# Moving PSUM evictions and a table's sign turns from VectorE to ScalarE, and one batch's stages by two slots, in a fused FFT filter and FFN kernel

## The chip, the cores and the metric

The kernel runs on one core of a Trainium2 chip. The metric is the device time in microseconds of one execution, as the median of several. TensorE, VectorE, ScalarE, GpSimd and SyncE are called PE, DVE, ACT, POOL and SP, as in the profile; L302 is line 302 of the kernel before.

## The reference

`x` is (8, 3008, 256): 8 batches, 3008 positions, 256 channels. Each channel is filtered along the positions by way of a Fourier transform, and each of the 24064 tokens then goes through a feed-forward layer:

```python
X = np.fft.rfft(x, axis=1)
Y = X * (filt_r + 1j * filt_i)[None, :, :]
y = np.fft.irfft(Y, n=3008, axis=1).reshape(24064, 256)
h = y @ w_in                                  # 256 x 2048
g = 0.5 * h * (1.0 + erf(h / np.sqrt(2.0)))
out = g @ w_out                               # 2048 x 256
```

## The kernel before

One class, `_Mix`, holds the tiles and the stages. The program writes the order of the instructions out by hand (`manual_schedule`): what is issued first stands first in the queue of its engine.

**The transform.** 3008 is split into 47 × 64, and each batch goes through two short transforms with tables on the partitions, the product with the filter between them, and two more short transforms. For batches 1 to 7 the stages are: `s1` (4 units; matmuls at L397, evictions into `a_sb`, a DMA to DRAM `R1`), `r1` (a DMA back as `b_sb`, L416), `s2` (12 units; matmuls at L424, and on DVE the product with the filter `F` into `p`, L427), `s3` (3 units; matmuls at L441 into four PSUM banks; `s3_out` evicts them into `v_sb`, two at once and two one slot later, and starts a DMA to `R2`), `r2` (a DMA back as `d_sb`) and `s4` (16 units: 8 groups `grp` by 2 halves; matmuls at L469, eviction into the ring `y_sb`). A stage takes PSUM banks from pool "f" (3 banks), a few from pool "h" (3 banks, shared with `mm1`).

**Evictions.** `_evac` (L299) copies a PSUM tile to SBUF: ACT where its argument is "act" (L302), else DVE (L304, or L306 with a factor). Before, `s3_out` gives the tile of `par` 0 to DVE and that of `par` 1 to ACT (L451); `s4` gives half 0 to DVE and half 1 to ACT (L474).

**The prologue** does batch 0 with stages of its own (`c1`, `c1t`, `c2`, `c3`, `c3t`, `c4`) and builds the tables. Table 3 has three quarters of eight columns, `q` 0 to 2. `table_3` transposes a quarter on PE into a PSUM bank, and `table_3_copy` lets ACT copy it to `T3`; a second table, `T3i`, is the same with its two parts swapped and signs turned by a per-partition factor (`turn_r`, `turn_i`). Before, quarters 0 and 1 get this from `table_3_turn` (L289: two DVE instructions that read `T3`), quarter 2 from ACT out of PSUM (L283). `c2` multiplies on DVE with the filter rows (L513); the rows on partitions 64 to 127 are copied there by `dup_filters` (L117), mostly on POOL. `c3` (L531) reads `T3` and `T3i`.

**The main loop** has 47 token tiles of 512 tokens, 16 slots each. In a slot stand, in this order: what `put` has entered for the slot, some matmuls of the second layer for the tile before (`mm2_seven`, L657), and one unit of the first layer (`mm1`: two matmuls, L584, and the GELU on ACT, L587). The second layer is done in seven products instead of eight, for which DVE adds and subtracts quarters of `g_sb` (`sums_1` L626, `sums_2` L632, `sums_3` L639) and puts the products together (L672 to L686).

In tile 5 (slots 80 to 95) batch 1's tokens begin during the tile, so its first six slots have no `mm1` but 14 matmuls of `mm2_seven` each, and the ten others hold all 16 `mm1`.

Where a batch's stages stand is given by a few numbers for each batch: `s1`, `r1`, `s2`, `r2`, `s4` are first slots, `n1`, `n2`, `n4` distances, `group` the distance between groups of four `s2` units. `hi` is the slot where the batch's tokens begin, 176 for batch 2.

```python
unit = lambda p: s2 + group * (p // 4) + int(n2 * (p % 4))
for p in range(12):
    put(unit(p), m.s2, b, p)
    if p % 4 == 3:
        put(unit(p) + 3, m.s3, b, p // 4)
        put(unit(p) + 4, m.s3_out, b, p // 4, 1)
```

`r1` of the last chunk follows the fourth unit of s2 by one slot, and the loads of the next batch's `x`, with a small POOL instruction (`gate`) that reads a `p`, stand in the slots of `s2` units.

Of the kernel before, what the change touches and what calls it, by code (L numbers as in the profile page):

```python
# [30 lines left out]
class _Mix:  # L31
# [244 lines left out]
    def table_3_copy(self, q, turn):  # L276

        k = slice(8 * q, 8 * q + 8)
        self._evac(self.T3[:, k], self.t3.rearrange("p (k w e) -> p k e w", k=8, e=4), "act")
        if turn:  # L280
            v = self.t3.rearrange("p (k w h r) -> p k h r w", k=8, h=2, r=2)
            for r in range(2):
                self._evac(self.T3i[:, k, r::2, :], v[:, :, :, 1 - r, :], "act", self.turn[r])  # L283
# [163 lines left out]
    def s3_out(self, b, u, i):  # L447
        ps = self.st[b, "ps3"][i]
        vt = self.pv.tile([128, 4, 256], BF16, tag="v", name="v_sb")
        for par in range(2):  # L450
            self._evac(vt[:, 2 * par:2 * par + 2, :].rearrange("p a b -> p (a b)"), ps[par], "act" if par else False)  # L451
        for q in range(2):
            self.nc.sync.dma_start(out=self.st[b, "R2"][:, 4 * u + 2 * i + q], in_=vt[64 * q:64 * q + 64])

# [8 lines left out]
    def s4(self, b, grp, half):  # L463
        nc = self.nc
        o = b % 2 * self.S
        d = self.st[b, "d", grp // 2]
        ps = self.bank("ps_s4")
        for i in range(4):
            nc.tensor.matmul(ps[:, 94 * i:94 * i + 94],  # L469
                             lhsT=d[:, (grp % 2) * 4 + i, 128 * half:128 * half + 128],  # L470
                             rhs=self.T4a[:, 4 * grp + i], start=True, stop=True)
        yv = self.ring[:, half, o:o + self.S].rearrange("c (m w) -> c m w", w=HB)[:, :, 4 * grp:4 * grp + 4]
        pv = ps[:, 0:376].rearrange("c (i m) -> c m i", i=4)
        self._evac(yv, pv, "act" if half else False, 1.0 / self.S)  # L474

# [163 lines left out]
    def mm2_seven(self, t, lo, hi):  # L641
# [5 lines left out]
        s31, s4 = self.st["s", t], self.st.get(("s4", t))  # L647
        ops = ((a11, w[:, 0, 0]), (a12, w[:, 1, 0]), (s2, q[:, 1]), (s31[:, :, 0], q[:, 2]),
               (s31[:, :, 1], q[:, 0]), (a22, q[:, 3]), (s4, w[:, 1, 1]))
        last = t == self.B * self.S // TCH - 1  # L650
        for n in range(lo, hi):
# [58 lines left out]
def kernel(  # L710
# [9 lines left out]
    m = _Mix(ctx, tc, x, filt_r, filt_i, moe_w_in, moe_w_out, out)  # L720
# [7 lines left out]
    act = "act"  # L728
# [35 lines left out]
    for u in range(16):  # L764
        m.c1(u // 2, u % 2, False if u in (1, 3, 5, 7, 8, 10, 12, 14) else act)
        if u == 3:
            m.warm_up(3)
            m.table_2_swap(0)
            m.table_2_angle(g, 1)
            m.T1q = g.tile([2 * NA, K1, 2, 2], BF16, name="T1q")  # L770
            nc.vector.tensor_copy(out=m.T1q, in_=m.T1.rearrange("p (h r k) -> p k h r", h=2, r=2))
        if u == 7:
            m.table_2_sin(1)
            m.table_3(0)
            m.table_3_copy(0, False)
            m.warm_up(2)
        if u == 11:
            m.table_2_swap(1)
            m.table_4(m.T4c, m.T1q, m.wtc, "n", False)
            m.table_3_turn(0)  # L780
            m.warm_up(1)
# [5 lines left out]
    for k in (12, 0):  # L787
        m.save_filters(k, 12)
    m.c1t(1, (act,))
    m.table_3_copy(1, False)  # L790
    m.c2(0)
    m.warm_up(1)
    m.c2(1)
    m.table_3_turn(1)
    m.c1t(2, (act,))
    m.warm_up(2)
    for q in range(1, 7):
        if q < 6:
            m.c2(2 * q)
            if q + 2 < 6:  # L800
                m.c1t(q + 2, (act,))
            if q != 3:
                m.warm_up(2)
            m.c2(2 * q + 1)
        if q < 6:
            m.c3(2 * q - 2)
            if q == 3:
                m.table_3(2)
                m.table_3_copy(2, True)
            else:  # L810
                m.warm_up(1)
        else:
            m.c3(10, 1)
            m.warm_up(1)
            m.c3(11, 1)
# [20 lines left out]
    def put(slot, f, *a):  # L836
        at.setdefault(slot, []).append((f, a))

    def first(b):
        return (b * S // TCH) * 16  # L840

    for b in range(1, B):
        hi = first(b)
        if b == 1:
            s1, n1, r1, s2, n2, group, r2, s4, n4 = 0, 3, 12, 27, 2.5, 12, 64, 73, 0.75
        elif b == 2:
            s1, n1, r1, s2, n2, group, r2, s4, n4 = hi - 90, 3.7, hi - 76, hi - 68, 3.4, 13, hi - 24, hi - 17, 1
        else:
            s1, n1, r1, s2, n2, group, r2, s4, n4 = hi - 94, 3.7, hi - 80, hi - 71, 3.4, 14, hi - 25, hi - 17, 1
        unit = lambda p: s2 + group * (p // 4) + int(n2 * (p % 4))  # L850
        for u in range(16):
            put(s4 + int(u * n4), m.s4, b, u // 2, u % 2)
        for c in range(4):
            put(s1 + int(c * n1), m.s1, b, c)
            put(r1 if c < 3 else unit(3) + 1, m.r1, b, c)
            put(r2 if c < 3 else s4 + int(4 * n4) + 1, m.r2, b, c)
# [5 lines that stand above are left out]
        if b + 1 < B:  # L862
            for i in range(8):
                put(unit(i + 2) if b > 1 else 25, m.load_next, b, i + 2, i // 2, i % 2)
# [63 lines left out]
```

## Time and profile before

| | |
|---|---|
| median of 8 runs | 752.89 us (752.03 to 753.77) |
| profiled execution | 752.75 us |
| its span | 751.0 us |
| busy PE, DVE, ACT, POOL | 730.3, 594.9, 543.6, 104.5 us |
| granted PE clock | 1.00 |

The profile is of one execution of the program on the chip. A row of a timeline has a start, a duration, the engine, the line, the operation, what it writes and reads, how many instructions stand in the row, and in brackets how long the engine was idle before it and which instruction ended that. Rows with "xN" are N instructions that followed each other; instructions of one engine overlap a little, so that the distance of two starts (the pitch) is shorter than a duration. The prologue ends and the main loop begins at about 39 us; slots 80 to 95 lie at about 112 to 131 us.

### The profile page before, as it was taken

To read this page: it belongs to the slowest core of one execution; us is meant where nothing else is said; L and a number is where in the kernel's file an instruction comes from. 1 tells how busy PE (TensorE), PEld (TensorE's weight loads), DVE (VectorE), ACT (ScalarE), POOL (GpSimd) and SP (SyncE) were. 2 spreads that over 40 slices of the span, in tenths; PEclk is the share of its full clock that TensorE was granted. 3 is DMA by queue.
4 is the path that set the end of the run, shared out by engine and by line. 5 is a ranking of instruction groups with operands and counts; after the bars stand their busy time and mean duration, and the time that the engine had idled before them with its cause. 6 is when DMAs were issued, how large, how long until landed. Compare 5 with 4: busy or idle time off the path is not lost.

```text
span 751.0 us, 20012 instructions
## 1 busy us (share of the span) xinstructions
PE 730.3 (97%) x8286; PEld 518.7 (69%) x8420; DVE 594.9 (79%) x1065; ACT 543.6 (72%) x963; POOL 104.5 (14%) x195
## 2 busy tenths in 40 slices
PE   8899999999999999999999999999999999999998
PEld 5756676666776767667677666666677766777776
DVE  8968977788787977789777997779967798666566
ACT  6896676767786677866777667876678767777773
POOL 7979100020001200012000120002100000000000
PEclk9999999999999999999999999999999999999999
DMA  9999752564544752547526457255562432501011
GB/s 147 219 223 238 154 142 78 161 126 115 112 112 144 151 120 78 142 136 134 126 81 170 109 110 166 57 152 120 121 146 72 135 106 76 123 29 58 30 57 58
DMA packets 90188, 90.71 MB, mean 121 GB/s; under 512 B 6768, under 2 KB 76912, under 8 KB 89840
## 3 DMA queue, kind: packets, MB, share of 16 engines
q1 hardware_dynamic: 82000, 72.18, 34.9%
q0 software_dynamic: 7680, 17.04, 14.4%
q8 instruction: 66, 1.08, 0.6%
q10 hardware_dynamic: 416, 0.20, 0.1%
q14 instruction: 26, 0.21, 0.1%
HBM read 57.15 MB, written 48.23 MB: 140 GB/s over the span
## 4 chain that ended last, share of the span: by engine, by line
PE 84%; DVE 8%; DMA 3%; ACT 2%; issue 2%; POOL 0%; SPq 0%; DVEq 0%; ACTq 0%; POOLq 0%
PE ps_o L657 35%; PE ps_h L584 35%; PE ps_s L469 3%; PE ps_s L424 2%; DVE p L427 2%; PE ps_s L441 2%; DVE s_sb L626 2%; PE ps_s L397 2%; ACT g_sb L587 2%; DMA R<-v_sb 1%; DMA d_sb<-R 1%; PE ps_o L598 1%; DVE g_sb L632 1%; DMA x_sb<-in_x_dram 1%; PE ps_c L531 1%
## 5 line engine op out<-in xcount | busy, mean ns | idle before, releaser
L587 ACT ACTIVATE g_sb<-ps_h 128x512 f16<-128x512 f32 x752 | 446.8, 599 | 182.7 <-PE ps_h L584 159.0
L584 PE MATMUL ps_h<-y_sb,w_in_sb 128*128 128x512 bf16 (+3 forms) x1470 | 417.3, 365 | 0.3
L657 PEld LDWEIGHTS <-g_sb 128*128 128x128 f16 x2944 | 193.9, 98 | 80.8 <-issue 15.2
L657 PEld LDWEIGHTS <-s_sb 128*128 128x128 f16 x2208 | 150.2, 98 | 51.2 <-issue 2.5
L657 PE MATMUL ps_o<-w_sums,g_sb 128*128 128x128 f16 x1472 | 127.8, 219 | 2.7 <-DVE g_sb L632 1.9
L584 PEld LDWEIGHTS <-w_in_sb 128*128 128x128 bf16 x1600 | 124.8, 98 | 8.1 <-issue 1.2
L657 PE MATMUL ps_o<-w_sums,s_sb 128*128 128x128 f16 x1472 | 125.8, 219 | 1.3
L626 DVE TENSOR_TENSOR s_sb<-g_sb 128x1024 f16<-128x1024 f16 x184 | 123.1, 692 | 0.3 <-ACT g_sb L587 0.3
L657 PE MATMUL ps_o<-w_out_sb,g_sb 128*128 128x128 f16 x1472 | 120.0, 219 | 1.8
L427 DVE TENSOR_TENSOR p<-ps_s,F 128x1024 bf16<-128x1024 f32 x84 | 102.6, 1221 | 16.6 <-PE ps_s L424 15.4
L122 POOL COPY gate<-p 1x1 bf16<-1x1 bf16 x40 | 18.3, 459 | 418.0 <-DVE p L427 418.0
L632 DVE TENSOR_TENSOR g_sb<-s_sb,g_sb 128x1024 f16<-128x1024 f16 x92 | 64.5, 701 | 1.1
L657 PE MATMUL ps_o<-w_out_sb,s_sb 128*128 128x128 f16 x736 | 63.8, 219 | 0.4
L639 DVE TENSOR_TENSOR s_sb<-g_sb 128x1024 f16<-128x1024 f16 x92 | 63.3, 688 | 0.0
L306 DVE TENSOR_SCALAR y_sb<-ps_s 128x376 bf16<-128x376 f32 x56 | 30.6, 546 | 28.2 <-PE ps_s L469 28.2
L679 DVE TENSOR_TENSOR t_sb<-t_sb,ps_o 128x256 f32<-128x256 f32 x46 | 19.2, 417 | 40.3 <-PE ps_o L657 40.2
L469 PEld LDWEIGHTS <-d_sb 96*128 96x128 bf16 x448 | 31.3, 98 | 25.4 <-issue 1.6
L304 DVE CAST a_sb<-ps_s 128x512 bf16<-128x512 f32 x57 | 36.6, 686 | 14.1 <-PE ps_s L397 13.9
L674 DVE TENSOR_TENSOR ost<-t_sb,ps_o 128x256 f32<-128x256 f32 x46 | 19.3, 419 | 32.4 <-PE ps_o L657 32.4
L469 PE MATMUL ps_s<-T4a,d_sb 96*128 96x94 bf16 x448 | 37.4, 206 | 1.9 <-DMA d_sb<-R 0.6
L686 DVE TENSOR_TENSOR ost<-t_sb,ps_o 128x256 f32<-128x256 f32 x90 | 33.6, 416 | 4.3 <-PE ps_o L657 4.3
L424 PE MATMUL ps_s<-b_sb,T2p 128*128 128x256 bf16 x168 | 32.1, 273 | 1.6 <-ACT v_sb L302 0.6
(148 smaller groups left out, 508.1 us busy)
## 6 DMA issues: line engine op xcount, KB each, us to landing
out_dram<-ost SPq DMA_DIRECT2D x92, 256.0 KB, 3.0
x_sb<-in_x_dram POOLq DMA_DIRECT2D x64, 188.0 KB, 3.7
b_sb<-R SPq DMA_DIRECT2D x28, 384.0 KB, 4.2
R<-v_sb SPq DMA_DIRECT2D x84, 128.0 KB, 2.5
d_sb<-R SPq DMA_DIRECT2D x56, 192.0 KB, 4.0
R<-a_sb SPq DMA_DIRECT2D x54, 192.0 KB, 3.1
F<-Fd SPq DMA_DIRECT2D x4, 512.0 KB, 10.0
Fd<-F SPq DMA_DIRECT2D x8, 192.0 KB, 6.1
```

The source lines that it names most:

```text
L304: self.nc.vector.tensor_copy(out=out, in_=in_)
L306: self.nc.vector.tensor_scalar(out=out, in0=in_, scalar1=scale, scalar2=None, op0=ALU.mult)
L424: nc.tensor.matmul(ps[:, 256 * i:256 * i + 256], lhsT=self.T2p[:, k].rearrange("p a b c d -> p (a b c d)"), rhs=self.st[b, "b", k // 6][:, ...
L427: nc.vector.tensor_tensor(out=w, in0=ps.unsqueeze(1).to_broadcast([128, 2, 512]), in1=self.F[:, :, 2 * p:2 * p + 2, :].rearrange("p t a b ...
L469: nc.tensor.matmul(ps[:, 94 * i:94 * i + 94], lhsT=d[:, (grp % 2) * 4 + i, 128 * half:128 * half + 128], rhs=self.T4a[:, 4 * grp + i], sta ...
L584: nc.tensor.matmul(ps[:, o:o + n], lhsT=w[:, dc], rhs=self.ring[:, dc, off:off + n], start=(dc == 0), stop=(dc == 1))
L587: nc.scalar.activation(out=self.st["g", t][:, jc, :], in_=ps, func=AF.Gelu)
L626: self.nc.vector.tensor_tensor(out=self.st["s", t][:, i:i + 2], in0=a, in1=b, op=ALU.subtract)
L632: self.nc.vector.tensor_tensor(out=a21[:, k], in0=self.st["s", t][:, k, 0], in1=a22[:, k], op=ALU.add)
L639: self.nc.vector.tensor_tensor(out=self.st["s4", t][:, k], in0=a12[:, k], in1=s2[:, k], op=ALU.subtract)
L657: nc.tensor.matmul(ps[:, (m + 1) % 2, sub, :], lhsT=a[:, i, 128 * sub:128 * sub + 128], rhs=b[:, i], start=i == 0, stop=i == 7)
L686: v(out=c(h, 1 - h), in0=tt, in1=p, op=ALU.add)
```

## The change

It has four parts.

1. Quarter 1 of the second table: `T3i` is no longer made by `table_3_turn(1)` on DVE. `table_3_copy(1, 2)` does it, with two ACT instructions that read the PSUM bank, as quarter 2 has them; they are issued behind the transposes and the eviction of `c1t(2)`, where the DVE instructions stood ahead of them.
2. In `s3_out`, batch 1's `par` 0 evictions (128x512, six of them) go to ACT.
3. In `s4`, batch 1's half 0 evictions of groups 4 to 7 (128x376, four of them) go to ACT.
4. Batch 2: `s1`, `r1` and `s2` begin two slots earlier (84, 98, 106 instead of 86, 100, 108), and `group` is 14 instead of 13. Its `s2` units stand in slots 106, 109, 112, 116, 120, 123, 126, 130, 134, 137, 140, 144, where they stood in 108, 111, 114, 118, 121, 124, 127, 131, 134, 137, 140, 144. `r2` and `s4` keep their slots.

```diff
     def table_3_copy(self, q, turn):
 
         k = slice(8 * q, 8 * q + 8)
-        self._evac(self.T3[:, k], self.t3.rearrange("p (k w e) -> p k e w", k=8, e=4), "act")
+        if turn < 2:
+            self._evac(self.T3[:, k], self.t3.rearrange("p (k w e) -> p k e w", k=8, e=4), "act")
         if turn:
...
         for par in range(2):
-            self._evac(vt[:, 2 * par:2 * par + 2, :].rearrange("p a b -> p (a b)"), ps[par], "act" if par else False)
+            self._evac(vt[:, 2 * par:2 * par + 2, :].rearrange("p a b -> p (a b)"), ps[par],
+                       "act" if par or b == 1 else False)
...
-        self._evac(yv, pv, "act" if half else False, 1.0 / self.S)
+        self._evac(yv, pv, "act" if half or b == 1 and grp > 3 else False, 1.0 / self.S)
...
-    m.table_3_copy(1, False)
+    m.table_3_copy(1, 0)
     m.c2(0)
     m.warm_up(1)
     m.c2(1)
-    m.table_3_turn(1)
     m.c1t(2, (act,))
+    m.table_3_copy(1, 2)
     m.warm_up(2)
...
         elif b == 2:
-            s1, n1, r1, s2, n2, group, r2, s4, n4 = hi - 90, 3.7, hi - 76, hi - 68, 3.4, 13, hi - 24, hi - 17, 1
+            s1, n1, r1, s2, n2, group, r2, s4, n4 = hi - 92, 3.7, hi - 78, hi - 70, 3.4, 14, hi - 24, hi - 17, 1
```

The other two calls of `table_3_copy` pass 0 and 1 where they passed False and True.

More of the change, by code (lines that the diff above doesn't have):

```diff
@@ L774 @@
             m.table_3(0)
-            m.table_3_copy(0, False)
+            m.table_3_copy(0, 0)
             m.warm_up(2)
@@ L808 @@
                 m.table_3(2)
-                m.table_3_copy(2, True)
+                m.table_3_copy(2, 1)
             else:
```

## The prediction

> **What bounds the kernel now.** I read the page's busy table first, then a table of busy time by stage, then PE's waits in the stages that the change touches, then each engine's timeline around every wait.
>
> ```profile
> PE 730.3 (97%) x8286; PEld 518.7 (69%) x8420; DVE 594.9 (79%) x1065; ACT 543.6 (72%) x963; POOL 104.5 (14%) x195
> ```
>
> PE is the bound: 97% of 751.0 us. Any gain has to come out of the 20.7 us in which PE stands idle. The stage table (us, then busy time of PE, PEld, DVE, ACT, POOL, clock, DMA share, GB/s):
>
> ```profile
> 61.00:103.00 42.00, 39.75 (x421) 26.90 (x427) 40.31 (x58) 26.99 (x48) 16.91 (x20) 1.00 0.73 169
> 103.00:120.00 17.00, 15.61 (x230) 12.99 (x231) 12.22 (x26) 10.46 (x20) 0.00 (x0) 1.00 0.43 117
> 120.00:137.00 17.00, 16.84 (x163) 9.43 (x164) 12.54 (x23) 14.78 (x29) 0.00 (x0) 1.00 0.49 124
> ```
>
> Batch 1's s2 and s3 lie in the first row (DVE 96%, ACT 64%), its s4 in the second, batch 2's s1 in the third (ACT 87%). PE's waits from 60 to 172 us (engine, tile, line, producer; total, times, longest):
>
> ```profile
> PE ps_o L657 <- DVE g_sb L632: 1.9, 3, 1.2
> PE ps_s L441 <- DVE p L427: 0.8, 1, 0.8
> PE ps_s L424 <- ACT v_sb L302: 0.6, 2, 0.3
> PE ps_s L441 <- ACT v_sb L302: 0.6, 1, 0.6
> ```
>
> These add up to 3.9 us, the prize of the main-loop parts. The largest, on PE's timeline (start, duration, instruction, idle before it):
>
> ```profile
> 116.09 0.39 PE L657 MATMUL ps_o<-w_sums,g_sb 128*128 128x128 f16 x4
> 117.71 0.51 PE L657 MATMUL ps_o<-w_sums,g_sb 128*128 128x128 f16 x6 [1.24 <-DVE g_sb L632]
> ```
>
> **Part 1, the turns of table quarter 1.** The two DVE turns become two ACT turns from PSUM, issued behind c1t(2). Their rows on DVE, and POOL beside them:
>
> ```profile
> 18.30 0.68 DVE L289 TENSOR_SCALAR T<-T,turn_r 128x512 bf16<-128x512 bf16 x1
> 18.91 1.12 DVE L289 TENSOR_SCALAR T<-T,turn_i 128x512 bf16<-128x512 bf16 x1
> ```
> ```profile
> 23.12 5.96 POOL L117 COPY F<-F 64x1024 bf16<-64x1024 bf16 x6 [1.21 <-DMA F<-in_filt_i_dram]
> ```
>
> DVE is back to back here, and from 18.30 to the next product at 19.95 the turns take 1.65 us. That is not the gain: each product also needs POOL's copy of its filter rows. The fifth copy starts at 23.12, when its DMA has landed, and ends about 5.96/6 = 0.99 us later, at 24.1; the product that needs it starts on DVE at 24.48. So some 0.3 us can be had, −0.3 (bounds 0 and −0.4). On ACT the form has rows in quarter 2 (27.57 and 28.14: a pitch of 0.57), so 1.14 us are added, ahead of c1t(3)'s eviction, behind c1t(2)'s. ACT waits 1.32 us ahead of its instruction at 22.16: covered. If that cover were gone the part would cost up to 0.3.
>
> The Trainium skill ("ScalarE: Activation LUTs", "Rules for kernel authors") speaks against parts 1 to 3: plain multiplies belong on VectorE, which per element is up to about three times as fast in bf16. The rows show the same where nothing disturbs DVE: quarter 0's turns took 0.34 and 0.36 us on DVE, quarter 2's 0.70 and 0.71 on ACT. By that rule the first part would lose about 0.7 us (an estimate from the page's rule and these rows); the sum goes by who is waited for instead.
>
> **Part 2, six v_sb evictions of batch 1 (128x512).** A DVE cast takes 684 ns, an ACT one 594. DVE gets about 6 × 0.60 = 3.6 us free between 71 and 103 us, but PE doesn't wait for DVE from 72 to 113 us: the 0.83 (L441 on p, 70.43) and 0.38 (L657 on g_sb, 71.60) come before the first moved cast (71.80) and stay. Direct gain: 0. The cost is on ACT. s3's second half takes a PSUM bank that the first half's par 1 holds, and waits for its eviction; that one now queues behind par 0's on ACT:
>
> ```profile
> 83.79 0.62 PE L441 MATMUL ps_s<-p,U 64*64 64x512 bf16 x7 [0.57 <-ACT v_sb L302]
> ```
>
> ACT's pitch for such an instruction is 0.48 (85.87 to 86.35). The group that already waits pays it in full, the others had slack: **+0.45** (bounds 0, all hidden, and +1.44, three groups at 0.48).
>
> **Part 3, four y_sb evictions of batch 1 (128x376).** DVE's queue ahead of the 1.24:
>
> ```profile
> 113.86 0.75 DVE L686 TENSOR_TENSOR ost<-t_sb,ps_o 128x256 f32<-128x256 f32 x2
> 114.52 0.54 DVE L306 TENSOR_SCALAR y_sb<-ps_s 128x376 bf16<-128x376 f32 x1
> 114.98 0.68 DVE L632 TENSOR_TENSOR g_sb<-s_sb,g_sb 128x1024 f16<-128x1024 f16 x1
> 115.58 0.68 DVE L626 TENSOR_TENSOR s_sb<-g_sb 128x1024 f16<-128x1024 f16 x1
> 116.18 0.42 DVE L672 COPY t_sb<-ps_o 128x256 f32<-128x256 f32 x1
> 116.52 0.54 DVE L306 TENSOR_SCALAR y_sb<-ps_s 128x376 bf16<-128x376 f32 x1
> 116.97 0.68 DVE L632 TENSOR_TENSOR g_sb<-s_sb,g_sb 128x1024 f16<-128x1024 f16 x1
> ```
>
> DVE runs without a gap from 112.80, and three of its y_sb (112.80, 114.52, 116.52), at a pitch of 0.46, stand ahead of the last sum. Without them it ends at 117.65 − 1.4 ≈ 116.25, and PE asks for it at about 116.3: −1.24 by the idle, −1.4 from start to start: the four matmuls at 116.09 would let the next begin at 116.31, and it begins at 117.71. I take **−1.4** (bounds −0.9, should one more instruction stand in DVE's queue, and −1.4). ACT has no GELU from 114 to 121 us and waits 0.54, 0.65 and 2.85 us ahead of its own y_sb: 4 × 0.46 fit. What is late next: batch 2's first s1, which now stands right behind the last s4 in slot 84; its bank waits for that unit's ACT eviction, **+0.25** (bounds 0 and +0.5, one eviction).
>
> **Part 4, batch 2 two slots earlier, groups of 14 slots.** With 13, two s2 fell into the slot of an s3 and waited for its ACT eviction (L424 on v_sb):
>
> ```profile
> 155.30 0.38 PE L424 MATMUL ps_s<-b_sb,T2p 128*128 128x256 bf16 x2 [0.29 <-ACT v_sb L302]
> 168.53 0.38 PE L424 MATMUL ps_s<-b_sb,T2p 128*128 128x256 bf16 x2 [0.34 <-ACT v_sb L302]
> ```
>
> With 14 the s3 is a slot ahead: start to start −0.36 and −0.41. The 0.31 before 150.39 (L657 on g_sb, 0.47 start to start) goes too, as one product of 1.22 us leaves DVE's queue ahead of that sum. Later batches, already at 14, still show a few tenths: at 239.25 seven matmuls take 0.80 where others take 0.55, and I charge one such 0.25. −1.24 + 0.25 = **−1.0** (bounds −0.5, the last sum still waiting, and −1.4, the 0.73 of seven matmuls at 163.35 back to 0.55 too). r1, r2, s4, the loads of x and POOL's gates move with their units; DMA share is 0.49 there, so I cost them at nothing; gone cover would show as a wait on b_sb or d_sb. s1's pairs of ACT evictions come in slots 84, 87, 91, 95 instead of 86, 89, 93, 97, of which 86 to 95 carry 1.6 GELUs each. ACT runs back to back there:
>
> ```profile
> 128.69 1.13 ACT L302 ACTIVATE a_sb<-ps_s 128x512 bf16<-128x512 f32 x2
> 129.64 3.30 ACT L587 ACTIVATE g_sb<-ps_h 128x512 f16<-128x512 f32 x6
> ```
>
> At least 16 GELUs and three pairs, 22 × 0.49 = 10.8 us, against PE's 10 or so in these slots. PE rides over it now on ps_h's spare banks, and the three pairs are as many as before (86, 89, 93), only later: +0 (bound +0.6, one GELU of 599 ns; more in the slower rival).
>
> **Sum.** −0.3 + 0.45 − 1.4 + 0.25 − 1.0 = −2.0. Against the profiled execution's 752.75 (span 751.0, 1.75 around it, which no part touches) that is 750.75; it lies 0.14 under the median of 752.89, so **750.9**. All ends at their best (−0.4, 0, −1.4, 0, −1.4) give −3.2, so 749.7.
>
> **The rivals.** *Half of it taken back*: ACT becomes the next wait. The turns give 0, two of the three s3 groups pay 0.48 (+0.96), the 1.24 goes only by 0.9, s1 pays 0.25, slots 86 to 95 cost 0.3, part 4 gives 1.0: −0.4, so 752.5. For it: s3 already waits 0.57 for v_sb. Against: ACT stands idle 1.64 us right behind that eviction, ahead of 85.38.
>
> *More*: all ends at their best, −3.2, 749.7, or below it, where the 3.6 us freed on DVE also shorten waits that I gave nothing. Against: PE's list has no DVE wait between 72 and 113.
>
> *Slower*: ACT sets the pace in slots 84 to 97. PE stops for ACT once ACT is later than two free ps_h banks, 2 × 0.51 = 1.0 us by PE's pitch for an mm1 with nothing between. Three pairs of s1 that find that used up cost PE 3 × 0.98 = 2.9; with three groups of v_sb (+1.44), s1's 0.25, and −0.3, −1.4, −1.0 kept: +1.9, so 754.8. It decides from all three pairs; with two it is 753.8, no change. For it: ACT at 87% from 120 to 137 us. Against: PE is busy 16.84 of 17.00 us there today with as many pairs.
>
> *It does nothing*: another producer stands right behind each that leaves, 752.9. Against: at 116.3 us nothing but DVE's sum is missing.
>
> **How the numbers follow.** Forecast 0.55, half taken back 0.25, more 0.08, slower 0.10, nothing 0.02. A measurement of this kernel tells about 0.2%, 1.5 us, from no change: faster is under 751.4, slower over 754.4. Faster 0.55 + 0.08 = 0.63, same 0.25 + 0.02 = 0.27, slower 0.10. The range reaches from 749.7 (all ends at their best; half of the *more* case lies below) to 752.6, the half-taken-back case with 0.1 to spare; above it remain the slower case and about 0.04 of tails, so some 0.18 is left out.
>
> **What would show it.** Right: PE's waits from 60 to 172 us lose L657's 1.24 and both L424 ones; L441 on v_sb grows to about 1.0; a short wait of s1 on y_sb appears near 119; the turns leave DVE and the main loop starts about 0.3 earlier. Wrong: new PE waits on g_sb of L587 between 119 and 132 us (ACT), or a wait on b_sb or d_sb.

## The result, and the profile after

The changed kernel takes 750.71 us (median of 10 runs, 750.34 to 751.68) against 753.12 us for the kernel before (28 runs): a ratio of 0.9971, 95% interval 0.9963 to 0.9979, so 2.4 us faster. The forecast was 750.9. The profiled execution took 751.30 us (its span 749.4), 1.45 less than the profiled execution before. Lines of the file shift by one to two (L441 is L442, L424 is L425, L469 is L471, L632 is L634, L657 is L659).

PE's waits between 60 and 172 us in the changed kernel:

```profile
PE ps_s L442 <- ACT v_sb L303: 1.0, 1, 1.0
PE ps_s L442 <- DVE p L428: 0.8, 1, 0.8
PE ps_s L471 <- DMA d_sb<-R: 0.8, 1, 0.8
PE ps_o L659 <- DVE g_sb L634: 0.4, 1, 0.4
```

Of the four lines of before, the 1.24 and the 0.31 on `g_sb` are gone, and so are both waits of s2 on `v_sb`. The wait of s3 on `v_sb` has grown from 0.57 to 1.02, as forecast. The third line is new and was in no step of the forecast: s4 waits for its `d_sb`. The forecast had named a wait on `d_sb` as a sign that it was wrong, so this one of its signs came, though at batch 1's s4 and not behind part 4, where it looked for it. The short wait of s1 near 119 us isn't a line of this list; it stands inside s1's row of eight matmuls, which takes 1.05 us where it took 0.63.

The stages (us, then busy PE, PEld, DVE, ACT, POOL, clock, DMA share, GB/s):

```profile
61.00:103.00 42.00, 39.31 (x418) 26.59 (x424) 36.64 (x52) 29.28 (x52) 16.63 (x20) 1.00 0.69 164
103.00:120.00 17.00, 16.01 (x226) 12.55 (x227) 10.80 (x23) 12.60 (x25) 0.00 (x0) 1.00 0.53 126
120.00:137.00 17.00, 16.84 (x166) 9.97 (x168) 12.12 (x23) 14.36 (x28) 0.00 (x0) 1.00 0.50 124
```

The first row is what part 2 does: DVE falls from 40.31 to 36.64 of 42 us, by the 3.6 that were worked out, and PE is no busier for it (39.31 against 39.75). The third row is the place of the slower rival: ACT has 14.36 of 17 us, and PE is at the same 16.84 as before.

Where PE stood 1.24 us before, it now goes on without a wait (PE, then the last sum on DVE):

```profile
117.11 0.73 PE L659 MATMUL ps_o<-w_sums,g_sb 128*128 128x128 f16 x10
```
```profile
116.59 0.68 DVE L634 TENSOR_TENSOR g_sb<-s_sb,g_sb 128x1024 f16<-128x1024 f16 x1
```

The prologue on DVE and POOL:

```profile
16.57 6.88 DVE L515 TENSOR_TENSOR p<-ps_c,F 128x1024 bf16<-128x1024 f32 x6 [0.47 <-PE ps_c L511]
23.87 5.75 DVE L515 TENSOR_TENSOR p<-ps_c,F 128x1024 bf16<-128x1024 f32 x5 [0.42 <-POOL F L117]
```
```profile
22.80 5.96 POOL L117 COPY F<-F 64x1024 bf16<-64x1024 bf16 x6 [1.21 <-DMA F<-in_filt_i_dram]
```

The turns have left the row of products, and the wait that the forecast put behind them is there in so many words: 0.42 us for POOL's copy of F, which had waited 1.21 us for its DMA.

Read at PE's first-layer matmuls of equal number, after against before, the difference is −0.59 us where the main loop starts, −0.39 from the first s2 on (its `b_sb` isn't there yet), +0.05 behind the s3 with the grown wait, +1.02 behind the new wait of s4, −0.38 at the last s4 (its own matmul of equal number: part 3 has given 1.40), about 0 behind batch 2's first s1, −1.40 from 169 us on.

### The profile page after: what moved, and what is told of

It reads as the page before. It is cut to its first block, busy times and chain, and to the rows that moved or that the text cites. A ratio compares the mean times of both kernels' runs of the same rounds, so it can differ in the third digit from the quotient of the medians.

```text
span 749.4 us, 20005 instructions
## 1 busy us (share of the span) xinstructions
PE 729.2 (97%) x8286; PEld 518.2 (69%) x8420; DVE 588.3 (79%) x1053; ACT 548.5 (73%) x975; POOL 105.1 (14%) x195
## 4 chain that ended last, share of the span: by engine, by line
PE 86%; DVE 6%; DMA 4%; ACT 2%; issue 2%; SPq 0%; POOL 0%; DVEq 0%; POOLq 0%; ACTq 0%
PE ps_o L659 36%; PE ps_h L586 36%; PE ps_s L471 3%; PE ps_s L442 3%; PE ps_s L425 3%; PE ps_s L398 2%; DVE p L428 2%; DVE s_sb L628 2%; ACT g_sb L589 2%; DMA R<-v_sb 1%; DMA d_sb<-R 1%; PE ps_o L600 1%; DMA x_sb<-in_x_dram 1%; PE ps_c L533 1%; DMA F<-in_filt_i_dram 1%
## 5 line engine op out<-in xcount | busy, mean ns | idle before, releaser
L659 PEld LDWEIGHTS <-g_sb 128*128 128x128 f16 x2944 | 193.9, 98 | 78.9 <-issue 14.8
L659 PEld LDWEIGHTS <-s_sb 128*128 128x128 f16 x2208 | 150.0, 98 | 51.6 <-issue 3.5
L659 PE MATMUL ps_o<-w_sums,g_sb 128*128 128x128 f16 x1472 | 127.3, 219 | 1.2 <-DVE g_sb L634 0.4
L659 PE MATMUL ps_o<-w_sums,s_sb 128*128 128x128 f16 x1472 | 125.8, 219 | 1.2
L659 PE MATMUL ps_o<-w_out_sb,g_sb 128*128 128x128 f16 x1472 | 119.8, 219 | 2.1 <-DVE ost L688 0.4
L634 DVE TENSOR_TENSOR g_sb<-s_sb,g_sb 128x1024 f16<-128x1024 f16 x92 | 64.5, 701 | 1.1
L659 PE MATMUL ps_o<-w_out_sb,s_sb 128*128 128x128 f16 x736 | 63.8, 219 | 0.5
L307 DVE TENSOR_SCALAR y_sb<-ps_s 128x376 bf16<-128x376 f32 x52 | 28.4, 546 | 27.3 <-PE ps_s L471 27.3
L471 PEld LDWEIGHTS <-d_sb 96*128 96x128 bf16 x448 | 31.3, 98 | 26.0 <-issue 1.9
L471 PE MATMUL ps_s<-T4a,d_sb 96*128 96x94 bf16 x448 | 37.4, 206 | 2.6 <-DMA d_sb<-R 1.2
L86 POOL DMA_DIRECT2D x_sb<-in_x_dram x64 | 32.9, 519 | 3.0 <-issue 2.9
```

What stands on the lines that cost most here:

```text
L86: nc.gpsimd.dma_start(out=xt[h * o:h * o + NA, w:w + 8, :], in_=xv[h][:, w:w + 8, :])
L307: self.nc.vector.tensor_scalar(out=out, in0=in_, scalar1=scale, scalar2=None, op0=ALU.mult)
L471: nc.tensor.matmul(ps[:, 94 * i:94 * i + 94], lhsT=d[:, (grp % 2) * 4 + i, 128 * half:128 * half + 128], rhs=self.T4a[:, 4 * grp + i], sta ...
L634: self.nc.vector.tensor_tensor(out=a21[:, k], in0=self.st["s", t][:, k, 0], in1=a22[:, k], op=ALU.add)
L659: nc.tensor.matmul(ps[:, (m + 1) % 2, sub, :], lhsT=a[:, i, 128 * sub:128 * sub + 128], rhs=b[:, i], start=i == 0, stop=i == 7)
```

## The experiments

The 95% intervals of the ratios to the kernel before are 0.6 to 1.1 us wide to either side, so a difference of medians well under 1 us isn't shown by the times alone; there the profiles say more. Single executions differ by over 1 us in their first 25 us alone (below).

**Each part undone.** In the changed kernel, `"act" if par or b == 1` back to `"act" if par` (no_v), `half or b == 1 and grp > 3` back to `half` (no_y), the line of batch 2 back (no_pace), and the turns on DVE again (no_turn).

> The changed kernel with part 2 undone: batch 1's par 0 tiles of v_sb go to DVE again. Theory (each part acts on its own wait, and part 2 only costs): L442's wait on v_sb at 82.8 us falls from 1.02 to about 0.57 (-0.45), and since the last v_sb write to R2 starts 0.48 earlier, the new 0.81 wait on d_sb at 106.3 shrinks by at least 0.5: 749.3 to 749.9 against the changed kernel's 750.71, about 3.3 under the kernel before. Rival (the 3.6 us freed on DVE are what lets part 3's sums be on time): the 1.24 on g_sb comes back in part and the time is 751 to 752.

749.58 us: 1.1 faster than the changed kernel, and the fastest of all, 0.9948 of before (0.9936 to 0.996). Part 2 costs 1.1 us. PE's waits from 60 to 172 us:

```profile
PE ps_s L442 <- DVE p L428: 0.8, 1, 0.8
PE ps_s L442 <- ACT v_sb L303: 0.6, 1, 0.6
PE ps_o L659 <- DVE g_sb L634: 0.4, 1, 0.4
PE ps_s L471 <- DMA d_sb<-R: 0.3, 1, 0.3
```

The wait on `v_sb` is at its old 0.57, the one on `d_sb` at 0.33 instead of 0.81, and no wait on `g_sb` has come back at 117 us: the rival, that part 3 needs the relief of part 2, is refuted.

> The changed kernel with part 3 undone: batch 1's half 0 tiles of y_sb in groups 4 to 7 go to DVE again. Theory: L659's wait on g_sb near 117 us comes back with 1.2 to 1.4 us, nothing else changes: 752.0. Rival (the sums are on time through part 2's relief of DVE alone): under 0.4 us of it comes back, 750.7 to 751.1. Second rival (the s4 evictions on ACT delay batch 2's first s1): that stall, 0.4 us in the row of eight at 118.9, goes as well, 751.6.

752.19 us, 1.5 over the changed kernel. The wait is back in its place and size:

```profile
PE ps_o L659 <- DVE g_sb L634: 1.6, 2, 1.2
```

So the first rival falls. The second falls too: s1's stall is still there, 0.40 us between the fifth and the sixth of its eight matmuls.

> The changed kernel with part 4 undone: batch 2 in slots 86, 100, 108 with groups of 13. Theory: the waits at 150 to 168 us come back (+1.4), s1's stall behind the last s4 goes (-0.36): 751.7. Rival (ACT between 120 and 131 us is what the earlier s1 costs or gains): PE shows waits on g_sb of ACT there, and the difference is under 0.5 or over 2.

751.47 us, +0.8 (theory +1.0). The waits at 150 to 168 us are back:

```profile
PE ps_o L659 <- DVE g_sb L634: 0.7, 2, 0.4
PE ps_s L425 <- ACT v_sb L303: 0.6, 2, 0.3
```

No wait on a GELU shows between 119 and 132 us, with or without part 4.

> The changed kernel with part 1 undone: quarter 1's turns on DVE again. Theory (the prologue's gain is cut twice, by POOL's copy and by the landing of b_sb at 58.7 us, which is issued at 55.27 in both traces): the main loop starts 0.3 to 1.1 later, but s2(1,0) later by 0.4 at most: 750.7 to 751.1. Rival (DVE's chain is the bound, the whole 1.65 counts): 751.8 to 752.4. Second rival (POOL's copies bind alone): no difference.

751.70 us, +1.0: below the range of the rival that gives the turns their whole 1.65, but far over the theory's 0.4. That expectation fell, and the next run is about it.

**Part 1 alone.** The kernel before with the turns on ACT.

> The kernel before with part 1 alone. The kernel with part 1 undone was 1.0 over the changed one, against the 0.3 of the forecast. Theory (POOL's fifth copy of F waits for its DMA, whose landing varies by 1 to 2 us between executions; where it lands earlier than in the first trace, the turns' time counts more fully): 1.0 under the kernel before, 752.1, and in the profile the product that needs the fifth copy starts 7.2 to 7.5 us after the first product, against 8.45 before. Rival (the 1.0 comes from a meeting of part 1 with the other parts): 0 to 0.4 under the kernel before, 752.7 to 753.1.

752.02 us, 1.04 under the 753.06 of before beside it. So the 1.0 belongs to part 1. The times in microseconds, read from the traces of all 14 kernels (some are described further down): the first product of the filter on DVE, how long DVE is idle ahead of the third, POOL's fifth copy (it starts when its DMA has landed, or behind the fourth), the product that needs it, and the distance of that product from the first:

| kernel | turns on | first product | wait of the third | fifth copy | its product | distance |
|---|---|---|---|---|---|---|
| before | DVE | 16.03 | 0 | 23.12 | 24.48 | 8.45 |
| no_turn | DVE | 16.10 | 0 | 22.01 | 24.87 | 8.77 |
| only_v | DVE | 15.89 | 0 | 21.66 | 24.29 | 8.40 |
| only_y | DVE | 16.52 | 0 | 23.15 | 24.71 | 8.19 |
| only_pace | DVE | 16.42 | 0 | 22.94 | 24.77 | 8.35 |
| after | ACT | 16.57 | 0 | 22.80 | 23.87 | 7.30 |
| no_v | ACT | 16.59 | 0.26 | 22.56 | 23.74 | 7.15 |
| no_y | ACT | 15.72 | 0.48 | 21.40 | 23.09 | 7.37 |
| no_pace | ACT | 16.26 | 0.55 | 23.83 | 24.90 | 8.64 |
| only_turn | ACT | 16.34 | 0.80 | 22.53 | 24.03 | 7.69 |
| par1_first | ACT | 16.04 | 0.53 | 22.12 | 23.46 | 7.42 |
| last_dve | ACT | 16.36 | 0.29 | 22.34 | 23.54 | 7.18 |
| best | ACT | 15.95 | 0.17 | 22.19 | 23.26 | 7.32 |
| late_s3 | ACT | 15.71 | 0.46 | 21.51 | 23.06 | 7.35 |

The fifth copy starts anywhere from 21.40 to 23.83. With the turns on DVE the distance is 8.2 to 8.8 wherever it starts: DVE runs without a gap from the first product to this one, so its own chain sets the distance. With the turns on ACT it is 7.15 to 7.7, except where the copy came at 23.83 (no_pace): that copy ends at 24.87, the product starts at 24.90, and the gain is gone. The averages, 8.43 and 7.49, are 0.94 apart, which fits the 1.0 of the medians; only_turn's own 7.69 lies a little over the 7.2 to 7.5 expected.

So the cap that the forecast saw is real, but the profile of before had one of the later fifth copies, and the cap was taken from it as if it were fixed. And there is another cap that the forecast didn't look at: six products back to back take 6 × 1.13 = 6.8 us, and no kernel has a distance as short. In eight of the nine kernels with the turns on ACT, the third product now waits 0.17 to 0.80 us, and starts 0.03 to 0.04 behind the end of POOL's first copy, which the turns had covered before (in late_s3, and at no_pace's 24.90, the profile names a PE matmul as what ended the wait, but the distance from the copy's end is the same 0.03):

```profile
19.21 6.88 DVE L515 TENSOR_TENSOR p<-ps_c,F 128x1024 bf16<-128x1024 f32 x6 [0.26 <-POOL F L117]
```

**Part 2 in pieces.** In the changed kernel, par 1 evicted first (`for par in ((1, 0) if b == 1 else (0, 1))`), and only the last of the six tiles back on DVE (`b == 1 and (u, i) != (2, 1)`).

> The changed kernel with batch 1's two v_sb evictions on ACT in the other order, par 1 first. Theory (L442 waits for par 1's bank, which stands behind par 0 on ACT): that wait falls from 1.02 to about 0.57, the d_sb wait stays at 0.8 to 0.9, since R2's write still waits for both: 750.3. Rival (the wait needs both banks): no difference, 1.02 stays.

750.22 us. The wait on `v_sb` is 0.54, as the theory says: s3 waits for par 1's bank, and part 2 had put par 0 ahead of it. The 0.31 left on `d_sb` isn't what was expected (0.8 to 0.9):

```profile
PE ps_s L442 <- ACT v_sb L303: 0.5, 1, 0.5
...
PE ps_s L471 <- DMA d_sb<-R: 0.3, 1, 0.3
```

> The changed kernel with only the last of the six par 0 tiles (group 2, second half) on DVE again. Theory (the d_sb wait comes from the last R2 write, 0.48 later by two evictions in a row on ACT): the d_sb wait falls by about 0.5, L442's 1.02 stays: 750.2. Rival (the d_sb wait is chance of the DMA): no difference, 750.7.

750.70 us, no difference by the medians (five runs, 749.34 to 751.55), where the theory said 0.5 and the rival, chance of the DMA, none: the times don't refute that rival. By the profile the wait on `d_sb` did fall to 0.33, with 1.02 left on `v_sb`:

```profile
PE ps_s L442 <- ACT v_sb L303: 1.0, 1, 1.0
...
PE ps_s L471 <- DMA d_sb<-R: 0.3, 1, 0.3
```

The chain behind it, in microseconds after the start of the last matmul of batch 1's s3, read from the traces (last write to R2 issued and landed; second read of the first `d_sb` issued and landed; PE's wait). Without a wait PE would start s4 at 10.19:

| kernel | last v_sb on | R2 issued | landed | d_sb issued | landed | wait |
|---|---|---|---|---|---|---|
| before | DVE, ACT | 2.95 | 5.40 | 5.84 | 9.91 | 0 |
| only_turn | DVE, ACT | 2.95 | 5.38 | 5.81 | 10.14 | 0 |
| no_v | DVE, ACT | 2.95 | 5.36 | 7.12 | 10.54 | 0.33 |
| best | DVE, ACT | 2.95 | 5.35 | 7.09 | 10.61 | 0.40 |
| last_dve | DVE, ACT | 2.95 | 5.36 | 7.07 | 10.54 | 0.33 |
| only_y | DVE, ACT | 2.95 | 5.35 | 7.09 | 10.60 | 0.38 |
| only_pace | DVE, ACT | 2.95 | 5.36 | 7.00 | 10.42 | 0.20 |
| late_s3 | DVE, ACT | 2.95 | 5.36 | 5.80 | 10.00 | 0 |
| after | ACT, ACT | 3.44 | 5.86 | 7.09 | 11.02 | 0.81 |
| no_y | ACT, ACT | 3.44 | 5.88 | 7.04 | 11.12 | 0.90 |
| only_v | ACT, ACT | 3.44 | 5.86 | 7.34 | 10.99 | 0.78 |
| no_turn | ACT, ACT | 3.44 | 5.85 | 6.29 | 11.16 | 0.94 |
| par1_first | ACT, ACT | 3.44 | 5.84 | 6.95 | 10.53 | 0.31 |
| no_pace | ACT, ACT | 3.44 | 5.84 | 6.97 | 10.50 | 0.28 |

Two evictions in a row on ACT start the write 0.49 later in every profile, and it lands 0.5 later. The read's landing is 9.91 to 10.61 with DVE and ACT side by side, 10.50 to 11.16 with ACT alone: the averages, 10.35 and 10.89, are 0.54 apart. In before the slack was 0.28 at most, and rather 0.14, as PE starts 0.14 behind the landing wherever it waits (landed at 11.02, started at 11.16 in after).

The later write is thus shown in all 14 profiles, but its effect on s4 only on average. Five kernels whose last pair is on DVE and ACT wait 0.20 to 0.40 as well, and two with the pair on ACT (par1_first, no_pace) wait no longer than those. The average waits are 0.20 and 0.67; the 0.47 between them and the 0.45 at s3's bank make 0.9 us of the 1.1 to 1.2 that part 2 costs.

**Parts 2, 3 and 4 alone**, each put into the kernel before.

> The kernel before with part 2 alone. Theory (part 2 only costs: 0.45 of L442's wait on v_sb, and about 0.5 of waiting on d_sb, as the last R2 write starts 0.49 later): 1.0 slower than the kernel before, 754.0, the wait on v_sb 1.02, a wait on d_sb of 0.3 to 0.9. Rival (the DVE time freed pays where part 3 hasn't already): L657's 1.24 on g_sb shrinks, and the time is 752.5 to 753.2.

754.41 us, 1.24 slower than before (ratio 1.0019, 1.0011 to 1.0028), with the wait on `g_sb` undiminished:

```profile
PE ps_o L659 <- DVE g_sb L634: 1.9, 3, 1.2
PE ps_s L442 <- ACT v_sb L303: 1.0, 1, 1.0
PE ps_s L442 <- DVE p L428: 0.8, 1, 0.8
PE ps_s L471 <- DMA d_sb<-R: 0.8, 1, 0.8
```

> The kernel before with part 3 alone. Theory (the whole 1.24 to 1.4 goes, and s1, still in slot 86, isn't stalled): 751.7, 1.4 under the kernel before. Rival (without the relief of part 2 DVE is late there all the same): 752.4 or more, and over 0.4 of the wait on g_sb is left.

751.10 us, 2.07 under before; the interval of the ratio (0.996 to 0.9982) reaches from 3.0 to 1.4. PE's list has no wait on `g_sb` near 117 us.

> The kernel before with part 4 alone. Theory (the 1.4 of waits at 150 to 168 us goes, and s1 in slot 84 pays 0.4 behind the last s4): 752.1, 1.0 under the kernel before. Rival (the waits move to other slots): waits of 0.3 or more on g_sb, p or v_sb between 130 and 172 us, 752.8 or more.

752.24 us, 0.93 under before, as the theory says. The waits at 150 to 168 us are gone, and none over 0.15 us has taken their place up to 172.

**Two steps further**, both from no_v: batch 2's s1 one slot later, `hi - 92` to `hi - 91` for s1 alone (best), and batch 1's first s3 one slot later, `put(unit(p) + 3 + (b == 1 and p == 3), ...)` (late_s3).

> The changed kernel without part 2 and with batch 2's s1 in slot 85 instead of 84 (85, 88, 92, 96). Theory (s1 in 84 stalls 0.36 to 0.42 behind the last s4's eviction): the row of eight L398 matmuls takes 0.63 instead of 1.05, and the time is 0.3 to 0.4 under the 749.58 without part 2, 749.2. Rival (the stall is paid again as ACT's pair of evictions meets the first GELUs of slot 86): no difference, 749.6.

749.69 us, no difference from 749.58. The stall of s1 behind the last s4 is gone, its eight matmuls take 0.63 instead of 1.05, but `b_sb` comes late for the first s2. The rival had the time right, but by another path:

```profile
118.04 0.63 PE L398 MATMUL ps_s<-x_sb,T1s 47*64 47x512 bf16 x8
```
```profile
PE ps_s L425 <- DMA b_sb<-R: 0.2, 1, 0.2
```

Half of the 0.4 is paid again there; the medians can't show the rest, and the rival's path, ACT's evictions against the first GELUs, shows no wait.

> The changed kernel without part 2, and batch 1's first s3 one slot later (38, its second half's eviction in 39). Theory (L442's 0.83 wait on p at 69 us is a product that DVE finishes late in the queue; a slot of 0.8 us covers it, and L659's 0.38 on g_sb right behind stays): -0.8, 748.8. Rival (DVE is the bound from 61 to 72 us, 96% busy, and the wait moves to the next sum): the 0.38 on g_sb grows to 1.0 or more, and the time is 749.5.

751.03 us, 1.4 slower than no_v, with the wait of s3 on `p` gone. The rival's mechanism holds, and costs more than it said (its 749.5). PE, then DVE:

```profile
70.17 0.51 PE L659 MATMUL ps_o<-w_sums,g_sb 128*128 128x128 f16 x6 [2.70 <-DVE g_sb L634]
```
```profile
65.16 1.42 DVE L634 TENSOR_TENSOR g_sb<-s_sb,g_sb 128x1024 f16<-128x1024 f16 x1
66.51 1.31 DVE L628 TENSOR_TENSOR s_sb<-g_sb 128x1024 f16<-128x1024 f16 x1
67.75 1.21 DVE L428 TENSOR_TENSOR p<-ps_s,F 128x1024 bf16<-128x1024 f32 x1
68.88 1.23 DVE L634 TENSOR_TENSOR g_sb<-s_sb,g_sb 128x1024 f16<-128x1024 f16 x1
```

DVE runs without a gap. s3's matmuls, about 1.0 us of PE, had covered part of DVE's time; now PE stands before the sum first and does them afterwards. By the profiles that loses 1.1 us: late_s3's first s2 starts 1.1 us ahead of no_v's (57.85 and 58.96), and at 72.4 us the two are level.

## Why the prediction was right, point by point

| term | forecast | trace after | undone | alone |
|---|---|---|---|---|
| 1, turns | −0.3 | −0.4 to −0.6 | −1.0 | −1.0 |
| 2, v_sb | +0.45 | +0.45 and +0.97 | +1.1 | +1.2 |
| 3, y_sb | −1.4 | −1.4 | −1.5 | −2.1 |
| 4, pace, with s1's stall | −0.75 | −1.0 | −0.8 | −0.9 |
| sum | −2.0 | 751.30 − 752.75 = −1.45 | −2.1 | −2.8 |

"Undone" is the changed kernel's 750.71 less the time without the part; "alone" is the part's difference from the kernel before, run beside it. The profile after shows less than the medians in part because that execution began late: its first product is at 16.57 against 16.03, behind a wait for x.

- Parts 3 and 4 went as worked out. With three `y_sb` out of the queue, DVE's last sum starts at 116.59 and ends at 117.27, and PE has no idle there; the waits on `v_sb` and `g_sb` at 150 to 168 us are gone. s1's stall was 0.36 to 0.42 (forecast 0.25, bound 0.5), and the 0.25 charged as a residual of part 4 wasn't paid.
- Part 1 was mis-sized, −0.3 for −1.0, outside its bounds of 0 and −0.4. The step that failed is the cap: one execution's fifth copy was read as the cap for all. Where it comes earlier, more of the turns' 1.65 counts, up to 1.3 (8.45 in before against 7.15 in no_v); POOL's first copy takes the rest, and the forecast didn't look at it.
- Part 2 was mis-sized too, +0.45 for +1.1. The 0.45 at s3's bank came exactly. What was missed is that an evicted tile doesn't end there: its write to R2, the read back, and s4 hang on it, and had 0.28 us of slack at most. The forecast followed r1, r2 and s4 for part 4 alone. Its bound of +1.44 holds the 1.1, but for three waits at s3's bank, of which there is one. That s4's share comes from the later write is shown on average only, and 0.2 to 0.3 of the cost isn't assigned.
- The two errors, −0.7 and +0.7, cancel: 750.9 was met partly by luck. The claim that DVE's freed 3.6 us buy nothing was right.
- The rivals: of *half taken back* the mechanism on ACT's `v_sb` is there, in one group and not in two. *Slower* is refuted, as PE has no wait on a GELU from 119 to 132 us. The rule of the Trainium skill ("ScalarE: Activation LUTs", "Rules for kernel authors"), which would have kept the multiplies of parts 1 and 3 on VectorE, fits the turns by the duration of one (0.34 us on DVE undisturbed, 0.70 to 0.84 on ACT), but not the time here: what counted was which queue PE was waiting for. The casts of part 2 it doesn't name. From PSUM ACT was the shorter anyway, 594 against 684 ns for a `v_sb` and 478 against 546 for a `y_sb`, which is a multiply.

Open: the second read of `d_sb` is issued 0.38 us behind the first in four profiles and 1.06 to 1.7 in the others, whatever part 2 does. No run tells why. Where it is 0.38 and DVE and ACT evict side by side, s4 starts within 0.1 us of its earliest.

## What to carry to other kernels

Move an eviction off a queue only where the profile names that queue as what PE waits for, and then follow the tile on to its last reader: here ten moved evictions of similar cost made −1.5 us (four of them, right ahead of a late sum) and +1.1 us (six: a PSUM bank came free later that s3 was waiting for, and their write and read back had 0.28 us of slack at most). Where a gain is capped by the landing of a DMA, one execution doesn't give the cap; keep the uncapped gain as the other bound. And the best of these kernels is the change without its second part: 749.58 us (the kernel called best, at 749.69, isn't told apart from it).

## What the runs showed that was not expected

The fifth copy of the filter, which waits for a DMA, starts up to 2.4 us apart in executions whose prologue has the same instructions (21.40 in no_y, 23.83 in no_pace). A DVE turn of 128x512 in bf16 that takes 0.34 us undisturbed took 0.68 and 1.12 beside POOL's copies, and 1.01 and 1.12 in no_turn. The turns on ACT, beside POOL's copies too, took 0.70 to 0.84 in the kernels before and after, at a pitch of 0.57 each time; what an undisturbed one takes there no run shows.
